# First batch of a Fourier filter: rows laid out from SBUF to SBUF, the last inverse rows moved straight to the first chunk's tile, ten crosswise filter steps by DMA

## The chip, the core and the metric

The kernel runs on one core of a Trainium2 chip. The metric is device time in microseconds (us), the median over the runs of one program. Engines are named as the profile names them: PE (matmuls), DVE (VectorE), ACT (ScalarE), POOL (GpSimd), SP (SyncE, which here only issues transfers). Transfers issued by SP and by ACT share the core's 16 DMA engines.

## The reference, cut to what matters

```python
def _attn_ref(x, filt_r, filt_i):                  # x: 8 x 3072 x 256
    X = np.fft.rfft(x, axis=1)
    Y = X * (filt_r + 1j * filt_i)[None]
    return np.fft.irfft(Y, n=x.shape[1], axis=1).astype(np.float32)

def _moe_ref(x, w_a, w_b, w_out):                  # d_ff = 1536
    return ((x @ w_a) * (x @ w_b) @ w_out).astype(np.float32)

reference = _moe_ref(_attn_ref(x).reshape(8 * 3072, 256), w_a, w_b, w_out)
```

The weights arrive as float64 and are converted to float32 parts on the chip, by integer work on DVE, ACT and POOL.

## The kernel before

A transform of length 3072 is done as 128 x 24. Forward stage one (`first_s1` in the first batch, `s1` later) multiplies by a 128-wide table for each of 24 columns n; the result is laid out anew so that a 24-point transform over n can run with (q, n) on 96 partitions; stage two (`first_s2`) does that transform and multiplies by the filter; the first inverse stage (`first_is1`) turns back; its rows go through a DRAM array `td` to a tile `tt`, in which 128 rows of one chunk stand together; the second inverse stage (`is2`) makes the first operand of the matrix part. Then the matrix part runs, six chunks a batch, with six visits (p) a chunk, and batches 1 to 7 have their transforms threaded between its matmuls. Only the first batch has nothing to hide behind: its transform stands in front of everything. The change touches this front.

The front in order. FRONT loads the table (`first_const`) and the input (`first_x`, six groups of four columns). `first_s1(i)`, i = 0 to 11, takes two columns each; eight of the twelve need their input split in two parts, `xh` by ACT and `xl` by POOL (`first_parts`). DVE copies each result back over the input tile (L526), and SP writes it to a DRAM array `z0` (L528, L530). `keep_warm` keeps PE busy with idle matmuls meanwhile. `between` then loads filters (`first_f`, 4 rows of 32 at a time, three tiles in turn) and reads `z0` back crosswise (`first_z`, eight groups g of four, six tiles in turn). The loop runs n = 0 to 18: `first_s2(n)` and, three steps behind, `first_is1(n-3)`. A step of `first_s2` multiplies its PSUM result by the filter (y) and by the filter with its two halves of 64 partitions exchanged (v). For nine of the 16 steps ACT makes the exchanged copy (`first_swap`, "w" in LOOP, two copies of 64 partitions); for the other seven DVE does v in two pieces (L584, L585). `first_is1` evicts by ACT (L598) and ACT stores pairs to `td` (L602, the last two one by one, L600). `first_tt` then loads `tt` by SP, two transfers for the first eight rows and two for the last eight.

The order of all this is written out by hand, engine by engine in program order: each engine and each issuing queue works through its own instructions in turn, and a wait blocks what stands behind it. The weight conversion is threaded in by the strings LOOP, TAIL, POST, LAST: for conversion number k, L loads raw words (SP), f takes the fields (DVE, L298, L299), p the power (ACT, L305, L306), s the sign (DVE, L311), g the high part (ACT, L318), l the low part (DVE, L321), v the value (POOL, L332), c the combination (POOL, L339), h the two float32 parts (ACT L350, POOL L351). Four raw tiles are used in turn.

A transfer raises one of eight completion semaphores, which are used in turn; an issue first waits for the earlier transfer on its own semaphore (`DMAHW0` to `DMAHW7` in the order rows).

Of the kernel before, what the change touches and what calls it, by code (L numbers as in the profile page):

```python
# [9 lines left out]
F32 = mybir.dt.float32  # L10
F32R = mybir.dt.float32r
# [9 lines left out]
NB = 32  # L21
# [64 lines left out]
def _tables():  # L86
# [98 lines left out]
    s1f = s1[[0, 12, *range(1, 12)]].transpose(1, 0, 2)  # L185
# [5 lines left out]
    for kind in range(2):  # L191
        for h in range(2):
            fi[64 * h:64 * h + 64, kind] = (1, -1)[h] * inv[kind, 0:64]
            fi[64 * h:64 * h + 64, 2 + kind] = inv[kind, 64:128]
    return [np.ascontiguousarray(a, np.float32) for a in (s1c, gc, fc, fl, ic, sc, s1f, ff, fi)]
# [23 lines left out]
def fft_filter_bilinear_kernel(ctx: ExitStack, tc, x, x0, filt, fny, filt0, fny0, wa, wb, wo, s1c, gc, fc, fl, ic, sc, s1f, ff, fi, out):  # L219
# [46 lines left out]
    def give_weights(p, where):  # L266
        wab[p] = [[where.tile([128, 7, 128], F32R, name=f"w{m}{h}{p}") for h in "hl"] for m in "ab"]

    for p in range(NP - LATE):
        give_weights(p, const)  # L270
    wo_h = [const.tile([128, 2, D], F32R, name=f"woh{p}") for p in range(NP)]
    wo_l = [const.tile([128, 2, D], F32R, name=f"wol{p}") for p in range(NP)]
# [6 lines left out]
    cut = pw.tile([128, 2], F32, name="cut")  # L279
    filts = [const.tile([128, 2, 2, D], F32, name=f"filt{i}") for i in range(2)]  # L280
# [85 lines left out]
    z0 = drc.tile([128, N2, D], F32, name="z0")  # L366
# [104 lines left out]
    def is1(b, i):  # L471
# [4 lines left out]
        nc.scalar.dma_start(out=td[b][i].rearrange("q n j d -> (q n) j d"), in_=t)  # L476


# [11 lines left out]
    def first_parts(i):  # L490
        g, h = divmod(i, 2)
        if i >= NI or i in WHOLE:
            return
        xt = held["x0", g][:, 2 * h:2 * h + 2]
# [6 lines left out]
    def first_x(g, parts=1):  # L501
        xt = fr.tile([128, 4, D], F32, name="x0", tag="in", bufs=6)
        xv = x0[:, 4 * g:4 * g + 4]
# [3 lines left out]
        held["x0", g] = xt  # L507

    BANKS = ((ps_h, "y"), (ps_h, "z"), (ps_o, "po0"), (ps_o, "po1"))

    def first_s1(i):
        g, h = divmod(i, 2)
        xt, sf = held["x0", g][:, 2 * h:2 * h + 2], held["sf"]
# [26 lines left out]
    def first_f(g):  # L540
        f = [*filts, more][g % 3].rearrange("p a n d -> p (a n) d")
        nc.sync.dma_start(out=f, in_=filt0[:, 4 * g:4 * g + 4])
# [479 lines left out]
```

## Time and profile before

| | us |
|---|---|
| median of 3 runs | 2463.68 (2462.14 to 2464.55) |
| the profiled execution | 2464.96 |
| its span, first to last instruction | 2463.2 |
| PE busy in the span | 2420.0 (98%) |
| DVE, ACT, POOL busy | 1780.7, 1405.0, 1223.0 |
| end of the last copy of stage one | 22.49 |
| start of the first matmul of `first_s2` | 30.39 |
| end of the last eviction of `first_is1` | 82.75 |
| start of the first eviction of `is2` | 90.00 |
| start of the matrix part's first matmul | 91.07 |

The page's 40 slices, of 61.6 us each, show PE at 70 to 89% in the first three and at 90% or more in all that follow. So the view to read is one by stages of the front, then the chain of waits through it, then the instructions in order of time.

### The profile page before, as it was taken

How to read it: one execution, taken by the hardware profiler on the slowest of the kernel's cores; microseconds unless marked ns; L12 is line 12 of the kernel's file. 1: busy time of each engine (PE TensorE's matmuls, PEld its weight loads, DVE VectorE, ACT ScalarE, POOL GpSimd, SP SyncE). 2: the span in 40 equal slices, each digit the busy share in tenths (PEclk: the TensorE clock that was granted, in tenths of full speed). 3: DMA queues.
4: the chain of work that ended last, by engine and by line, in shares of the span. 5: the costliest groups of instructions: out<-in, count | busy, mean ns of one | idle time of the engine just before them, and what ended most of it. 6: DMA issues, size and time to landing. Idle time of an engine off the chain costs nothing.

```text
span 2463.2 us, 46508 instructions
## 1 busy us (share of the span) xinstructions
PE 2420.0 (98%) x17478; PEld 2263.9 (92%) x17478; DVE 1780.7 (72%) x2511; ACT 1405.0 (57%) x2480; POOL 1223.0 (50%) x926
## 2 busy tenths in 40 slices
PE   7889999999999999999999999999999999999999
PEld 3588999999999999999999999999999999999998
DVE  6775996569955798568976589656996569955554
ACT  5755555555556555565555555565555655555454
POOL 4765454545545554454545545454454545534333
PEclk9999999999999999999999999999999999999999
DMA  9437442544334443245523454145432444310100
GB/s 303 160 127 239 148 134 71 171 143 142 116 102 142 152 154 114 88 146 160 159 80 112 157 158 139 63 145 166 142 121 78 161 144 149 108 39 22 44 22 18
DMA packets 209397, 310.21 MB, mean 126 GB/s; under 512 B 19186, under 2 KB 119476, under 8 KB 209092
## 3 DMA queue, kind: packets, MB, share of 16 engines
q1 hardware_dynamic: 166580, 230.55, 30.3%
q10 hardware_dynamic: 42592, 76.70, 8.9%
q8 instruction: 137, 2.24, 0.4%
q14 instruction: 88, 0.72, 0.1%
HBM read 202.31 MB, written 108.45 MB: 126 GB/s over the span
## 4 chain that ended last, share of the span: by engine, by line
PE 93%; DMA 2%; issue 2%; ACT 1%; DVE 1%; POOL 1%; SPq 0%; ACTq 0%; POOLq 0%; DVEq 0%
PE x L226 30%; PE po L226 30%; PE z L226 15%; PE y L226 7%; PE ps L635 3%; PE ps L226 3%; PE ps L441 2%; PE ps L442 2%; DMA filt<-in_filt 1%; PE ps L556 0%; POOL xl L393 0%; PE ps L524 0%; DMA zf<-z 0%; DVE g L678 0%; DMA gt<-in_gc 0%
## 5 line engine op out<-in xcount | busy, mean ns | idle before, releaser
L687 POOL TENSOR_TENSOR gl<-g,gh 128x512 fp32r<-128x512 f32 x574 | 745.1, 1301 | 788.8 <-ACT gh L686 762.5
L678 DVE TENSOR_TENSOR g<-c 128x512 f32<-128x512 f32 x576 | 509.1, 884 | 271.1 <-ACT c L968 134.0
L968 ACT COPY c<-x 128x512 f32<-128x512 f32 x288 | 169.2, 587 | 688.0 <-PE x L226 685.1
L686 ACT CAST gh<-g 128x512 fp32r<-128x512 f32 x576 | 357.1, 620 | 52.8 <-PE po L226 26.7
L226 PE MATMUL po<-gh,woh 128*128 128x512 f32 x1152 | 369.5, 388 | 2.6 <-DVE filt L706 2.6
L226 PE MATMUL po<-gl,woh 128*128 128x512 f32 x1152 | 359.8, 380 | 0.0
L226 PE MATMUL po<-gh,wol 128*128 128x512 f32 x1152 | 359.8, 380 | 0.0
L226 PE MATMUL x<-ah,wah 128*128 128x256 f32 x1152 | 316.8, 275 | 7.0 <-ACT c L932 4.5
L226 PE MATMUL x<-al,wah 128*128 128x256 f32 x1152 | 317.1, 275 | 0.1
L226 PE MATMUL x<-ah,wal 128*128 128x256 f32 x1152 | 316.9, 275 | 0.0
L226 PE MATMUL x<-ah,wbh 128*128 128x256 f32 x1152 | 316.9, 275 | 0.0
L226 PE MATMUL x<-al,wbh 128*128 128x256 f32 x1152 | 316.9, 275 | 0.0
L226 PE MATMUL x<-ah,wbl 128*128 128x256 f32 x1152 | 316.9, 275 | 0.0
L957 DVE TENSOR_TENSOR c<-x,c 128x512 f32<-128x512 f32 x288 | 197.9, 687 | 155.3 <-PE x L226 149.9
L226 PEld LDWEIGHTS po<-gl,woh 128*128 128x128 f32 x1152 | 217.3, 189 | 32.6 <-DVE gl L687 0.4
L226 PEld LDWEIGHTS po<-gh,wol 128*128 128x128 f32 x1152 | 218.3, 190 | 29.3
L226 PEld LDWEIGHTS x<-ah,wah 128*128 128x128 f32 x1152 | 219.5, 191 | 26.0 <-ACT c L932 5.9
L226 PEld LDWEIGHTS x<-al,wah 128*128 128x128 f32 x1152 | 219.6, 191 | 15.3 <-DVE al L646 0.3
L656 POOL TENSOR_TENSOR al<-t,ah 128x512 fp32r<-128x512 f32 x96 | 146.3, 1544 | 152.3 <-ACT ah L655 152.3
L226 PEld LDWEIGHTS x<-ah,wal 128*128 128x128 f32 x1152 | 221.3, 192 | 0.0
L226 PEld LDWEIGHTS x<-ah,wbh 128*128 128x128 f32 x1152 | 221.3, 192 | 0.0
L226 PEld LDWEIGHTS x<-al,wbh 128*128 128x128 f32 x1152 | 221.3, 192 | 0.0
(145 smaller groups left out, 6067.4 us busy)
## 6 DMA issues: line engine op xcount, KB each, us to landing
z<-zh ACTq DMA_DIRECT2D x112, 256.0 KB, 2.5
filt<-in_filt SPq DMA_DIRECT2D x112, 256.0 KB, 2.6
zth<-z SPq DMA_DIRECT2D x112, 256.0 KB, 3.0
tt<-td SPq DMA_DIRECT2D x94, 256.0 KB, 3.9
out<-ot SPq DMA_DIRECT2D x47, 512.0 KB, 3.0
td<-t ACTq DMA_DIRECT2D x114, 192.0 KB, 2.1
xt<-in_x SPq DMA_DIRECT2D x84, 256.0 KB, 4.2
st<-s1d SPq DMA_DIRECT2D x84, 256.0 KB, 2.7
```

Of the source, the lines that this page charges most:

```text
L226: nc.tensor.matmul(out, w, m, **kw)
L441: nc.tensor.matmul(out, w[:, 0], hi, start=True, stop=False)
L442: nc.tensor.matmul(out, wl[:, 0], lo, start=False, stop=True)
L635: nc.tensor.matmul(to, tt[:, n, 128 * k:128 * k + 128], gt[:, n].rearrange("p (k a) -> p k a", k=2), start=True, stop=True)
L656: nc.gpsimd.tensor_tensor(out=al[:, 3 + i:5 + i], in0=t[:, i:i + 2], in1=f32(ah[:, 3 + i:5 + i]), op=ALU.subtract)
L678: nc.vector.tensor_tensor(out=gt, in0=g[:, :, 0], in1=g[:, :, 1], op=ALU.mult)
L686: nc.scalar.copy(out=gh, in_=gt)
L687: low.tensor_tensor(out=gl, in0=gt, in1=f32(gh), op=ALU.subtract)
L957: nc.vector.tensor_tensor(out=c1[:, 1], in0=bx, in1=c1[:, 1], op=ALU.add)
L968: nc.scalar.copy(out=c1[:, 0], in_=bx)
```

## The change

- `first_z` no longer reads `z0`, which is gone. The input tile is one tile, `first_in`, of 24 columns, and group g is filled by four transfers from SBUF to SBUF, each from 4 partitions (24 columns of 1 KB) to 96 partitions of 1 KB: 32 transfers, all issued after the last copy of stage one. For g = 0 and 1 every second one is issued by ACT, the rest by SP. The targets are weight tiles that aren't written yet (`zs`). The columns of the stage one table are permuted on the host so that the four partitions of a transfer stand 32 apart.
- The exchanged filter is needed for all 16 steps: steps 0 to 5 by ACT as before, steps 6 to 15 by a transfer of 256 KB from a filter array with a third block of 64 rows (`first_w`), three buffers in turn. The seven steps with two pieces on DVE are gone.
- `first_is1` keeps its rows, from the third pair on, in columns of `first_in`, and the rows of `td` are ordered by chunk (in all batches; `load_td` reads them so). For steps 12 to 15 the 16 rows of chunk 0 go by two small transfers each straight into `tt`, without `td`; only steps 8 to 11 are left for the second `first_tt`.
- Smaller: ACT's table is loaded ahead of the data (`warm`); the pieces of the table load are 4, 4 and 5 columns instead of 3, 5 and 5; two filters are loaded before the first raw words; `keep_warm` 8 and 6 become 4 and 5; "f1 p1" moves from before the loop into its step 0; "h6" moves from TAIL to step 16 of the loop; the first low part in `is2` of chunk 0 goes from POOL to DVE.

```diff
-    s1f = s1[[0, 12, *range(1, 12)]].transpose(1, 0, 2)
+    s1f = s1[[0, 12, *range(1, 12)]].reshape(13, N1, 8, 4, 4).transpose(1, 0, 4, 3, 2).reshape(N1, 13, 128)
...
+    zs = [f32(whole).rearrange("p m h k f -> p (m h k f)")[:, 1024 * i:1024 * (i + 1)].rearrange("p (j d) -> p j d", d=D) for i in range(3)]
+    zs += [f32(t).rearrange("p h f d -> p (h f) d") for t in wo_b[:0:-1]]
...
-        td[b] = dr.tile([NJ, 4, N2, 2, D], F32, name="td", tag="td")
+        td[b] = dr.tile([NJ, NC, 4, 4, 2, D], F32, name="td", tag="td")
...
         nc.vector.tensor_copy(out=xt, in_=ps)
-        if g == NI // 2 - 1:
-            nc.sync.dma_start(out=z0[:, 2 * i:2 * i + 2], in_=xt)
-        elif h:
-            nc.sync.dma_start(out=z0[:, 4 * g:4 * g + 4], in_=held.pop(("x0", g)))
...
-    def first_z(g, parts=1):
-        zt = fr.tile([128, 4, D], F32, name="zf", tag="in", bufs=6)
-        zv = z0.rearrange("(j q) n d -> j (q n) d", q=4)[4 * g:4 * g + 4].rearrange("j p d -> p j d")
-        for n in range(parts):
-            part = slice(4 * n // parts, 4 * (n + 1) // parts)
-            nc.sync.dma_start(out=zt[0:96, part], in_=zv[:, part])
+    def first_z(g):
+        queues = (nc.sync, nc.scalar if g < 2 else nc.sync)
+        zt = zs[g]
+        zv = first_in.rearrange("(q m g) n d -> g m q n d", m=4, g=8)[g]
+        for m in range(4):
+            queues[m % 2].dma_start(out=zt[0:96, m], in_=zv[m])
...
+    def first_w(i):
+        if not swapped:
+            swapped.append(p2.tile([128, 3, 2, D], F32, name="fs", tag="al"))
         g, h = divmod(i, 2)
+        w = held["w", i] = swapped[0][:, i % 3]
+        if i < SWAPPED:
+            for a, b in ((0, 64), (64, 0)):
+                nc.scalar.copy(out=w[a:a + 64], in_=held["f0", g][b:b + 64, 2 * h:2 * h + 2])
+        else:
+            nc.sync.dma_start(out=w, in_=filt0[64:192, 2 * i:2 * i + 2])
...
-            nc.vector.tensor_tensor(out=v[0:64], in0=ps[64:128], in1=f[0:64], op=ALU.mult)
-            nc.vector.tensor_tensor(out=v[64:128], in0=ps[0:64], in1=f[64:128], op=ALU.mult)
+        nc.vector.tensor_tensor(out=v, in0=ps, in1=held.pop(("w", i)), op=ALU.mult)
...
+            if g < 2:
+                held["t0"] = fr.tile([96, 2, 2, D], F32, name="t0", tag="t")
+            else:
+                held["t0"] = first_in[0:96, 4 * g - 8:4 * g - 4].rearrange("p (h j) d -> p h j d", h=2)
...
+        near = 16 if i >= DIRECT else 0
+        if near:
+            tt = held["t", 0, 0][0][8 * i:8 * i + 8].rearrange("(q j) n d -> j q n d", j=2)
+            for j, queue in enumerate((nc.sync, nc.scalar if i == NJ - 1 else nc.sync)):
+                queue.dma_start(out=tt[j], in_=t[0:16, h, j])
...
+        between = [(lz, 0), (lz, 1), (steps, BETWEEN), (first_w, 0), (first_w, 1), load, (lz, 2), (lf, 2), (first_w, 2), (lz, 3), load, (lz, 4), load, (lz, 5), (lz, 6), (lz, 7)]
+        ISSUE = {0: ((first_w, 3),), 1: ((lf, 3), (first_w, 4),), 2: ((first_w, 5),), 3: ((first_w, 6), (lf, 4),), 4: ((first_w, 7),), 5: ((first_w, 8), (lf, 5),), 6: ((first_w, 9),), 7: ((first_w, 10), (lf, 6),), 8: ((first_w, 11),), 9: ((first_w, 12), (lf, 7),), 10: ((first_w, 13),), 11: ((first_w, 14),), 12: ((first_w, 15),)}
```

SP's queue where stage one ends, before: `z_122` is the DRAM array `z0`, `zf` the tile that is read back, `filt_118` a filter tile, `raw` the weight words. The writes end, and the reads wait for all of them.

```order
L528 DMA z_122<-x_150 128x512 [waits DMAHW5_49,DVE_49]
L528 DMA z_122<-x_150 128x512 [waits DMAHW6_49,DVE_49]
L288 DMA raw<-in_wb 128x2x512 [waits DMAHW7_49]
L542 DMA filt_118<-in_filt 128x1024 [waits DMAHW0_49]
L550 DMA zf<-z_122 96x2x256 [waits DMAHW4_49,DMAHW3_49,DMAHW5_49,DMAHW2_49,DMAHW6_49,DMAHW1_49,PE_49]
L550 DMA zf<-z_122 96x2x256
L542 DMA filt_119<-in_filt 128x1024
```

SP's queue now, at the end of the 32 transfers (`x_109` is `first_in`, `wo_88` a weight tile, `fs` the exchanged filter):

```order
L550 DMA wo_88<-x_109 96x1x256 [waits DMAHW3_49]
L550 DMA wo_88<-x_109 96x1x256 [waits DMAHW4_49]
L550 DMA wo_88<-x_109 96x1x256 [waits DMAHW5_49]
L550 DMA wo_88<-x_109 96x1x256 [waits DMAHW6_49]
L542 DMA filt_101<-in_filt 128x1024 [waits DMAHW7_49,DVE_49,Activation_49]
L569 DMA fs<-in_filt 128x512 [waits DMAHW0_49,DVE_49,Activation_49]
L542 DMA filt_102<-in_filt 128x1024 [waits DMAHW1_49]
L569 DMA fs<-in_filt 128x512 [waits DMAHW2_49,DVE_49,Activation_49]
L294 DMA raw<-in_wo 128x2x512 [waits DMAHW3_49]
```

The write and the read have become one transfer each, and the filter of group 3 (`filt_101`) and all exchanged filters by DMA stand behind the last of them.

ACT in the loop about step 7, before: exchanged copies (L569) stand among the evictions (L598).

```order
L598 COPY t_403<-ps 96x512 [waits PE_49]
L602 DMA td<-t_403 96x2x512 [waits DMAHW2_49,Activation_49]
L569 COPY fs<-filt_119 64x512 [waits DMAHW6_49]
L569 COPY fs<-filt_119 64x512
L318 ACTIVATE sc<-t 128x512 [waits DVE_49]
L305 ACTIVATE sc<-sc,cut 128x512 [waits DVE_49]
L306 ACTIVATE sc<-sc,cut 128x512 [waits Activation_49]
L598 COPY t_453<-ps 96x512 [waits DMAHW5_49,PE_49]
```

ACT at the same place now:

```order
L596 COPY t_390<-ps 96x512 [waits PE_49]
L603 DMA td<-t_390 96x2x512 [waits DMAHW4_49,Activation_49]
L324 ACTIVATE sc<-t 128x512 [waits DVE_49]
L311 ACTIVATE sc<-sc,cut 128x512 [waits DVE_49]
L312 ACTIVATE sc<-sc,cut 128x512 [waits Activation_49]
L596 COPY x_109<-ps 96x512 [waits DMAHW5_49,DMAHW3_49,DMAHW6_49,DMAHW1_49,DMAHW7_49,DMAHW0_49,PE_49]
L596 COPY x_109<-ps 96x512 [waits PE_49]
```

The copies are gone, and the eviction of step 4 of `first_is1`, which writes into `first_in`, waits for transfers out of it on six semaphores.

ACT where the front ends, before: the last evictions, each with a store to `td`, then "h6" (two casts) and the conversions of TAIL.

```order
L598 COPY t_647<-ps 96x512 [waits PE_49]
L600 DMA td<-t_647 96x512 [waits Activation_49]
L350 CAST wah_91<-m 128x896 [waits Pool_49]
L350 CAST wbh_93<-m 128x896
L318 ACTIVATE sc<-t 128x512 [waits DVE_49]
L305 ACTIVATE sc<-sc,cut 128x512 [waits DVE_49]
L306 ACTIVATE sc<-sc,cut 128x512 [waits Activation_49]
L318 ACTIVATE sc<-t 128x512 [waits DVE_49]
L350 CAST woh_100<-t 128x512 [waits Pool_49]
```

ACT at the same place now:

```order
L596 COPY x_109<-ps 96x512 [waits PE_49] x2
L601 DMA tt<-x_109 4x4x256 [waits DMAHW2_49,Activation_49]
L603 DMA td<-x_109 80x2x512 [waits DMAHW4_49]
L324 ACTIVATE sc<-t 128x512 [waits DVE_49]
L311 ACTIVATE sc<-sc,cut 128x512 [waits DVE_49]
L312 ACTIVATE sc<-sc,cut 128x512 [waits Activation_49]
L324 ACTIVATE sc<-t 128x512 [waits DVE_49]
L356 CAST wo_88<-t 128x512 [waits Pool_49]
```

The transfer into `tt` comes straight behind the last eviction, and the two casts of "h6" stand earlier in the program.

## Rows read from the trace of the kernel before

**Rows 1.** Windows by stage: stretch, length, engine busy us (instructions), PE clock, DMA share, GB/s.

```profile
core 0: us, PE busy (x) PEld busy (x) DVE busy (x) ACT busy (x) POOL busy (x), PEclk, DMA share, GB/s
0.00:22.50 22.50, 13.74 (x34) 8.33 (x34) 10.38 (x19) 7.26 (x13) 10.69 (x12) 1.00 0.87 319
22.50:30.40 7.90, 7.14 (x17) 2.97 (x17) 2.62 (x5) 3.78 (x6) 0.00 (x0) 1.00 1.03 312
30.40:50.00 19.60, 14.94 (x39) 6.33 (x39) 16.50 (x27) 10.95 (x20) 5.36 (x6) 1.00 1.07 293
50.00:66.00 16.00, 14.38 (x33) 5.32 (x34) 15.80 (x24) 12.59 (x21) 13.55 (x10) 1.00 0.98 296
66.00:82.75 16.75, 15.23 (x36) 5.73 (x35) 15.65 (x27) 13.61 (x24) 9.91 (x10) 1.00 0.73 226
82.75:91.10 8.35, 6.27 (x27) 3.41 (x25) 2.77 (x6) 5.73 (x11) 6.58 (x4) 1.00 0.62 199
91.10:130.00 38.90, 32.86 (x222) 29.47 (x223) 30.60 (x51) 25.69 (x46) 28.24 (x19) 0.96 0.41 143
```

**Rows 2.** The chain that ended last, in order of time: start us, us, what.

```profile
22.51 2.98 DMA z<-x
25.56 4.79 DMA zf<-z
...
36.23 10.01 DMA filt<-in_filt
...
82.78 2.13 DMA td<-t
...
85.69 3.00 DMA tt<-td
...
90.00 0.59 ACT x L643
...
93.29 1.28 POOL al L656
```

**Rows 3.** Timeline, stage one: start us, us, engine, line, operation, count, idle before.

```profile
7.16 1.28 ACT L487 ACT_TABLE_LOAD   x1 [7.16 <-DMA sf<-in_s1f]
...
8.66 0.35 SPq L808 DMA_DIRECT2D icf<-in_fi  x1
...
9.46 10.48 POOL L498 TENSOR_TENSOR xl<-x,xh 128x512 fp32r<-128x512 f32 x8 [9.02 <-ACT xh L497]
...
17.48 5.01 DVE L526 COPY x<-ps 128x512 f32<-128x512 f32 x7
```

**Rows 4.** Timeline, from the end of stage one to the last eviction.

```profile
22.40 0.69 DVE L298 TENSOR_SCALAR sc<-raw 128x512 int32<-128x512 int32 x1
...
23.81 0.66 ACT L306 ACTIVATE sc<-sc,cut 128x512 int32<-128x512 f32 x1
...
30.39 2.08 PE L556 MATMUL ps<-zf,fcf 96*128 96x256 f32 x6 [0.72 <-DMA zf<-z]
...
48.64 0.68 DVE L580 TENSOR_TENSOR y<-ps,filt 128x512 f32<-128x512 f32 x1
...
82.17 0.58 ACT L598 COPY t<-ps 96x512 f32<-96x512 f32 x1 [0.40 <-PE ps L556]
```

**Rows 5.** Groups by line in 30.4 to 82.75: busy us, mean ns, idle before.

```profile
L569 ACT COPY fs<-filt 64x512 f32<-64x512 f32 x14 | 8.6, 617 | 5.9 <-DMA filt<-in_filt 5.4 <-ACT t L598 0.4
...
L585 DVE TENSOR_TENSOR v<-ps,filt 64x512 f32<-64x512 f32 x5 | 3.4, 683 | 0.1
```

**Rows 6.** SP's issues of the reads of `z0`: ns min/median/max, first and last start.

```profile
L550 SPq DMA_DIRECT2D zf<-z x9: 342/432/465, 25.6 to 62.0; - x9
```

**Rows 7.** DMA queues in 300 to 2300 us: packets, MB, share of 16 engines' time.

```profile
q1 hardware_dynamic: 136800, 179.68, 29.3%
q10 hardware_dynamic: 36176, 65.09, 9.3%
```

More of the change, by code (lines that the diff above doesn't have):

```diff
@@ L194, in _tables @@
             fi[64 * h:64 * h + 64, 2 + kind] = inv[kind, 64:128]
+    ic, fi = (a.reshape(*a.shape[:-1], 4, NC, 4).swapaxes(-3, -2).reshape(a.shape) for a in (ic, fi))
     return [np.ascontiguousarray(a, np.float32) for a in (s1c, gc, fc, fl, ic, sc, s1f, ff, fi)]
@@ L266, in give_weights @@
     def give_weights(p, where):
-        wab[p] = [[where.tile([128, 7, 128], F32R, name=f"w{m}{h}{p}") for h in "hl"] for m in "ab"]
+        whole = where.tile([128, 2, 2, 7, 128], F32R, name=f"wab{p}")
+        wab[p] = [[whole[:, m, h] for h in range(2)] for m in range(2)]
+        return whole
     for p in range(NP - LATE):
-        give_weights(p, const)
-    wo_h = [const.tile([128, 2, D], F32R, name=f"woh{p}") for p in range(NP)]
-    wo_l = [const.tile([128, 2, D], F32R, name=f"wol{p}") for p in range(NP)]
+        whole = give_weights(p, const)
+    wo_b = [const.tile([128, 2, 2, D], F32R, name=f"wo{p}") for p in range(NP)]
+    wo_h, wo_l = ([t[:, h] for t in wo_b] for h in range(2))
+    zs = [f32(whole).rearrange("p m h k f -> p (m h k f)")[:, 1024 * i:1024 * (i + 1)].rearrange("p (j d) -> p j d", d=D) for i in range(3)]
+    zs += [f32(t).rearrange("p h f d -> p (h f) d") for t in wo_b[:0:-1]]
     fct = const.tile([128, 3, 128], F32R, name="fct")
@@ L279, in fft_filter_bilinear_kernel @@
     cut = pw.tile([128, 2], F32, name="cut")
+    warm = pw.tile([128, 2], F32, name="warm")
     filts = [const.tile([128, 2, 2, D], F32, name=f"filt{i}") for i in range(2)]
@@ L556, in first_turn @@
                 nc.tensor.matmul(ps[:, j0:j1], w[q][:, kind], m[:, j0:j1], start=q == 0, stop=q == len(ins) - 1)
-    swapped = {}
-    def first_swap(i):
+    swapped, SWAPPED = [], 6
+    def first_w(i):
+        if not swapped:
+            swapped.append(p2.tile([128, 3, 2, D], F32, name="fs", tag="al"))
         g, h = divmod(i, 2)
-        f = held["f0", g][:, 2 * h:2 * h + 2]
-        if not swapped:
-            swapped["w"] = p2.tile([128, 3, 2, D], F32, name="fs", tag="al")
-        w = held["w", i] = swapped["w"][:, len(swapped) % 3]
-        swapped[i] = True
-        for a, b in ((0, 64), (64, 0)):
-            nc.scalar.copy(out=w[a:a + 64], in_=f[b:b + 64])
+        w = held["w", i] = swapped[0][:, i % 3]
[4 more added lines that the diff above has]
+            nc.sync.dma_start(out=w, in_=filt0[64:192, 2 * i:2 * i + 2])
     def first_s2(i):
@@ L787, in steps @@
                     load_weights()
-                elif what[0] == "w":
-                    first_swap(int(what[1:]))
                 else:
@@ L823, in fft_filter_bilinear_kernel @@
         nc.vector.memset(cut[:, 1:2], float(255 << 23))
+        nc.scalar.copy(out=warm, in_=cut)
         for what, *args in FRONT:
@@ L841, in fft_filter_bilinear_kernel @@
                 first_s2(n)
-            if n % 2 and n // 2 + 3 < NJ // 2:
-                first_z(n // 2 + 3)
-            if n % 2 and n // 2 + 3 < NJ // 2:
-                first_f(n // 2 + 3)
+            for what, *args in ISSUE.get(n, ()):
+                what(*args)
             if n >= 3:
```

91 lines of the change are left out of this document (44 added, 47 removed).

## The prediction, made before the changed kernel was run

> **What bounds the kernel now.** I read the page first: PE is busy 98% of the span, so only the front before the matrix part has time to give. The windows by stage [rows 1] say how much: in the first 91.1 us PE misses 8.8 us in stage one, 0.8 between the stages (filled with idle matmuls, so that stretch is 7.9 us without any use), 7.8 us in the loop (4.7 + 1.6 + 1.5) and 2.1 plus some 5 us of idle matmuls at its end. Next the chain of waits in order of time [rows 2]. It has four places: the write of `z0` and its reading back (2.98 and 4.79 us), waits for filters in the loop (the longest 10.01 us), the store to `td` and the load of `tt` (2.13 and 3.00 us), and the split in `is2` by POOL (1.28 us). Last the timeline, for what stands ahead of each. In the loop no engine is free: of 52.4 us (30.4 to 82.75) DVE works 48.0, PE 44.6, and the DMA engines are at a share of about 1 until 66 [rows 1]. So the loop hangs on several limits at once, and taking one away gives little more than the distance to the next.
>
> **The change, part by part.** The sum is made against the profiled execution, 2464.96 us, which lies 1.28 above the median of the three runs.
>
> *Stage one.* POOL's eight splits run as one block of 10.48 us from 9.46, which starts late: ACT's first cast waits for the second table piece until 7.16 and then for 1.28 us of table load [rows 3]. Now the table is loaded ahead, and the first cast needs only the first piece. The first split goes ahead, but the second needs input group 1; the issue of `icf` that waits for it starts at 8.66 [rows 3]. With one copy of about 0.6 us on ACT the second split starts at 9.3 instead of 9.46 + 1.31 = 10.77. That is 1.5 us for the whole block. Bounds: 1.2 (only the load is saved) and 2.9 (if group 1 doesn't hold it). Stage one then ends at 21.0, not 22.49 (17.48 + 5.01, rows 3).
>
> *The layout.* Before, 7.9 us from the last copy to 30.39. Now two transfers must land for step 0, one from SP, at once, and one from ACT, which first does the power of conversion 0: DVE's fields at 22.40, ACT's second ACTIVATE over at 24.47 [rows 4], 2.0 us after the last copy. An issue by SP takes 0.43 us [rows 6], and a landing lies between the 2.13 us of the `td` store and the 2.98 of the `z0` write [rows 2], so it is 2.0 + 2.1 to 3.0, with the issue 4.1 to 5.4. I take 4.5: step 0 at 25.5. This saves 3.4 us (2.5 to 3.8).
>
> *The loop.* DVE loses seven instructions of 0.683 us, 4.8 us [rows 5]; "f1" comes into the loop with about 1.1. ACT loses six of 18 copies of 0.617, 3.7 us, and the 11 us in which its queue stood still for filters, of which 5.4 is in the row [rows 5]. So by DVE the loop shrinks by 3.7 us to 48.7. What takes some of it back: SP's queue. Behind stage one stand 28 transfers, three weight loads and a filter, 32 issues of 0.43 us = 13.8 us, or nearer 18 if an issue from four partitions takes longer than the row's longest. Filter 3 is issued at 35 to 39 and lands, like the loads in the chain, up to 10.01 us later [rows 2]; y of step 6 wants it at about 42 (48.64 in rows 4, less 4.9, less some). I count 0 to 5 us, and take 1.7. Exchanged filters have three buffers, so each has three steps to arrive in; PE's share of a step is 44.6/16 = 2.8 us, three are 8.4 us, and most landings fit into it. Loop: 2.0 us saved (-3 to +6).
>
> *The end.* From the last eviction's end, 82.75 [rows 4], to ACT's first eviction of `is2` at 90.00 [rows 2] is 7.25 us: store, load, matmuls. Now one transfer stands there, 0.6 + 2.1 to 3.0, and 1.2 us of matmuls: 3.9 to 4.8. But ACT itself has two issues (0.6), four conversion steps of about 0.6 to 0.66 and a cast of 0.6 before that eviction, with a sign on DVE (0.69) between: 4.4 us. I take 4.4, saved 2.8 (1.0 if a conversion is late, 3.4 if none is). "h6" costs nothing in the loop: its 1.9 us on ACT take the room of the copies; without them ACT would be later by that much at the end.
>
> *`is2`.* The low part by DVE takes 0.7 us, not POOL's 1.28 [rows 2]: 0.6 us. The new order of `td` leaves pieces of 1 KB as they were: nothing, and the visits hide the loads in any case.
>
> *After it* conversions and matrix part keep their order, so the shift is handed on. From 91.1 to 130 PE works 32.9 of 38.9 us beside a DVE at 30.6 and POOL at 28.2 [rows 1]; an earlier start could lose or win 2 us there.
>
> Sum: 1.5 + 3.4 + 2.0 + 2.8 + 0.6 = 10.3 us. 2464.96 - 10.3 - 1.28 = 2453.4; I say **2453.5**. With the bounds the forecast's own range is 2445 to 2460.
>
> **The rivals.**
>
> *Slower: the 32 transfers run on a part of the DMA engines.* Each has only four source partitions. The large transfers of the front have 32 to 128 rows on both sides, so no row shows what four do. If only four of 16 engines work on them, 3072 packets of 1 KB are 768 for each. The two queues took 0.293 x 16 x 2000/136800 = 68.5 ns for a packet of 1.31 KB and 0.093 x 16 x 2000/36176 = 82 ns for 1.80 KB [rows 7], scaled 47 to 53 ns a KB; at the loop's load, a share of 1.07 at 293 GB/s [rows 1], 60 ns. So 36 to 46 us, and 6 to 7 more for the 2 MB of weights and filter between (at about 300 GB/s), from 21.0 to 63 to 74. Two things stand behind the last: filter 3 in SP's queue, for y of step 6, and ACT's eviction of step 4 in `first_is1`, into the tile that is still read. At 53 ns step 6 has its y at about 69 instead of 48.64. After it PE has some ten inverse and nine forward steps, 27 us with waits, so the last eviction ends at 96 instead of 82.75. Less 3.4 us for the end and `is2`, that is 10 us lost: 2474 (47 to 60 ns, with waits: 2467 to 2485). It decides from some 40 us for the layout: up to there the loop's own pace hides it.
>
> This is also what the Trainium skill says. "DMA: Bandwidth & Descriptors", in the section on why a DMA increments its semaphore by 16, has a transfer use the largest number of engines, up to 16, that divides the slowest dimension of both sides; of 4 and 96 that is 4, and always the same ones. By that rule this rival is the forecast and the time 2474. The trace can't say: it has no transfer of such a shape.
>
> For the rival: the shape is new, and both waits are in the order. Against it: no row shows a transfer on a part of the engines, the reads of 1 KB and the weights between the stages come at 312 GB/s together [rows 1], and even 40 us of transfers would be read in time by a loop of 50 us, were it not for what is queued behind. I give it 0.25.
>
> *No difference: DVE waits for the exchanged filters.* ACT's copies are replaced by ten transfers of 256 KB in a stretch where DMA is at a share of 0.98 to 1.07 [rows 1], and a load can take 10.01 us to land [rows 2]. With three buffers a step then takes (10.0 + 0.4 + 0.7)/3 = 3.7 us, not 2.8; over ten steps 9 us, which is the gain of the other parts: 2463, and the bytes are the same 293 GB/s that the loop had. It decides from a landing of about 7.3 us on. For it: the sum of bytes hardly falls, `z0` moved twice and now once, but 2.6 MB of filters come. Against it: the layout is over by the time the exchanged filters begin, and then the 1 KB reads are gone from the mix. I give it 0.15.
>
> *It doesn't do what it says* would be a wait left on the old path; the order shows none, and I give that nothing of its own.
>
> **How the numbers follow.** Forecast 0.60, slower rival 0.25, no difference 0.15. A measurement of this kernel can tell about 0.2%, 4.9 us. The forecast lies beyond that but for its upper end; what it gives up there the second rival's lower side gives back. So faster 0.60, same 0.15, slower 0.25. A range for 8 in 10 reaches from the forecast's lower end, 2445, into the slower rival until half of it is in: **2445 to 2476**.
>
> **What would show it.** Right: first split at about 6.5 and stage one over by 21; first matmul of `first_s2` at 25 to 26; all 32 transfers landed by 40 and eviction of step 4 not waiting for them; `is2`'s first eviction within 5 us of the last one of `first_is1`, at 79 to 81 instead of 90.0. The slower rival would show as a landing of the last layout transfer beyond 60, DMA share near 0.25 to 0.5 while they run, and PE, DVE and ACT idle together about steps 4 to 6. The second rival would show as DVE waiting for `fs` at every step. The forecast is wrong, with all of that right, if the matrix part from 91 to 260 us later takes back what it got.

## The result: 2487.66 us, slower by 0.93%, and the profile after

The changed kernel takes 2487.66 us (median of 4 runs, 2483.97 to 2489.75) against 2464.11 for the kernel before beside it: a ratio of 1.0093, 95% interval 1.0076 to 1.0109, 23.5 us lost. The forecast was 2453.5 and its range ended at 2476. The side it came out on is that of the slower rival, priced at 2474. The profiled run took 2488.81 us, with a span of 2487.0. Two of the nine runs of experiment 8 below came in a slow state, at 3117 and 3574 us, and the median given there is that of the other seven.

First the windows by stage of the kernel after; columns as in [rows 1], cut where its own stages change.

```profile
core 0: us, PE busy (x) PEld busy (x) DVE busy (x) ACT busy (x) POOL busy (x), PEclk, DMA share, GB/s
0.00:22.00 22.00, 14.57 (x34) 8.41 (x34) 11.34 (x19) 7.74 (x14) 10.70 (x12) 1.00 0.77 267
22.00:26.00 4.00, 3.70 (x8) 1.44 (x8) 1.57 (x3) 1.32 (x2) 0.00 (x0) 1.00 0.16 31
26.00:34.00 8.00, 2.56 (x6) 1.10 (x6) 1.81 (x3) 5.16 (x9) 0.00 (x0) 0.74 0.43 124
34.00:38.00 4.00, 2.52 (x4) 0.50 (x2) 0.84 (x2) 0.51 (x2) 0.00 (x0) 0.50 0.27 95
38.00:52.00 14.00, 9.12 (x19) 4.19 (x18) 5.13 (x10) 3.03 (x6) 1.27 (x1) 0.74 0.55 167
52.00:56.00 4.00, 0.97 (x2) 0.40 (x3) 4.00 (x7) 3.39 (x6) 2.12 (x3) 0.50 0.28 97
56.00:66.00 10.00, 10.00 (x20) 3.86 (x18) 2.67 (x5) 4.68 (x7) 7.54 (x6) 0.77 0.43 134
66.00:82.75 16.75, 4.97 (x9) 1.66 (x8) 7.29 (x13) 3.60 (x7) 2.26 (x3) 0.64 0.91 310
82.75:91.10 8.35, 8.35 (x19) 3.38 (x18) 8.09 (x14) 6.47 (x10) 7.30 (x6) 0.90 0.95 318
```

In [rows 1] the DMA engines are at a share of 0.98 to 1.07 and 293 to 312 GB/s from 22.5 to 66. Here they are at 0.27 and 95 GB/s where hardly anything but the row transfers runs (34 to 38, 52 to 56): 0.27 x 16 is 4.3 engines. A share of 0.27 at 95 GB/s is 46 ns for a packet of 1 KB on one engine, so the engines that work are not slow; the others have nothing to do. PE pays twice: it works 5.0 of 16.75 us in 66 to 82.75 (15.2 before), and where it has waited its granted clock is at 0.50, the 1.2 GHz level (34 to 38, 52 to 56).

The issues of the row transfers (duration in ns as min/median/max, then first and last start):

```profile
L550 SPq DMA_DIRECT2D wo<-x x20: 520/1012/2442, 38.2 to 62.7; - x20
L550 SPq DMA_DIRECT2D wab<-x x8: 519/626/1736, 22.0 to 37.1; - x8
L550 ACTq DMA_DIRECT2D wab<-x x4: 539/1426/1847, 23.3 to 26.8; - x4
```

The issue of a read of `z0` took 432 ns [rows 6]; these take 1012 as a median for the later ones: SP's queue goes at the pace of the four engines (run 5 shows this by itself). The last is issued at 62.7. Then the chain that ended last (start, us, what):

```profile
26.72 10.38 DMA raw<-in_wb
...
62.75 0.79 SPq L550
...
63.65 0.87 SPq L542
...
67.05 10.29 DMA raw<-in_wo
77.44 0.71 DVE sc L304
78.17 0.67 ACT sc L311
...
79.46 0.59 ACT x L596
80.09 21.30 PE ps L556 x44
...
105.91 1.07 ACT x L596 x2
107.00 0.74 ACTq L601
...
109.05 2.37 DMA tt<-x
...
111.51 3.55 PE ps L642 x16
```

Filter 3 is issued at 63.65 behind the last transfer, and step 6 gets its product at 71.76 (48.64 in [rows 4]), after DVE has waited 13.1 us for that filter. Behind the filters in SP's queue the weights `in_wo` are issued at 67.05 and land 10.29 us later; DVE's and ACT's conversion of them stands ahead of ACT's eviction of step 4 (L596, 79.46), for which PE has waited 12 us. From 80.09 on all is there, and the loop runs through in 26.9 us. Its last eviction ends at 106.97, not 82.75; the first of `is2` starts at 113.38, not 90.00. That is 23.4 us, and the whole program is 23.5 us longer.

### The profile page after: what moved, and what is told of

Its sections match the earlier page's. It is cut to its first block, busy times and chain, and to the rows that moved or that the text cites. A ratio compares the mean times of both kernels' runs of the same rounds, so it can differ in the third digit from the quotient of the medians.

```text
span 2487.0 us, 46522 instructions
## 1 busy us (share of the span) xinstructions
PE 2426.3 (98%) x17468; PEld 2267.5 (91%) x17468; DVE 1778.0 (71%) x2505; ACT 1402.5 (56%) x2475; POOL 1221.6 (49%) x925
## 4 chain that ended last, share of the span: by engine, by line
PE 92%; DMA 2%; DVE 2%; SPq 1%; ACT 1%; issue 1%; POOL 1%; ACTq 0%; POOLq 0%; DVEq 0%
PE x L227 30%; PE po L227 29%; PE z L227 15%; PE y L227 7%; PE ps L642 3%; PE ps L227 3%; PE ps L446 2%; PE ps L447 2%; SPq L550 1%; PE ps L556 1%; DMA raw<-in_wb 0%; DMA raw<-in_wo 0%; POOL xl L398 0%; DMA x<-in_x 0%; DVE g L686 0%
## 5 line engine op out<-in xcount | busy, mean ns | idle before, releaser
L227 PE MATMUL x<-ah,wab 128*128 128x256 f32 x4608 | 914.4, 275 | 6.8 <-ACT c L940 4.6
L227 PEld LDWEIGHTS x<-ah,wab 128*128 128x128 f32 x4608 | 768.5, 192 | 25.4 <-ACT c L940 5.7
L227 PE MATMUL x<-al,wab 128*128 128x256 f32 x2304 | 634.2, 275 | 0.0
L227 PE MATMUL po<-gh,wo 128*128 128x512 f32 x2304 | 618.2, 384 | 1.9 <-DVE filt L714 1.9
L227 PE MATMUL z<-ah,wab 128*128 128x256 f32 x2304 | 481.0, 275 | 0.3 <-ACT ah L662 0.3
L227 PEld LDWEIGHTS x<-al,wab 128*128 128x128 f32 x2304 | 441.3, 192 | 15.1
L227 PEld LDWEIGHTS po<-gh,wo 128*128 128x128 f32 x2304 | 407.0, 190 | 46.3 <-DVE filt L714 2.1
L227 PEld LDWEIGHTS z<-ah,wab 128*128 128x128 f32 x2304 | 396.6, 192 | 0.8 <-ACT ah L662 0.7
L694 ACT CAST gh<-g 128x512 fp32r<-128x512 f32 x576 | 357.0, 620 | 52.2 <-PE po L227 26.7
L227 PE MATMUL po<-gl,wo 128*128 128x512 f32 x1152 | 359.5, 380 | 0.0
L227 PE MATMUL z<-al,wab 128*128 128x256 f32 x1152 | 317.4, 276 | 2.3 <-POOL al L664 1.9
```

Source lines behind the costliest of these rows:

```text
L227: nc.tensor.matmul(out, w, m, **kw)
L694: nc.scalar.copy(out=gh, in_=gt)
```

## The experiments

Each ratio is to the kernel before on the same chip, with its 95% interval in brackets. A table at the end of this section sets the profiles side by side.

**1. The layout undone alone.** Row order, `z0` and its writes and reads as in the kernel before, into the change's tiles:

```diff
+            nc.sync.dma_start(out=z0[:, 2 * i - 2:2 * i + 2], in_=first_in[:, 2 * i - 2:2 * i + 2])
...
-        for m in range(4):
-            queues[m % 2].dma_start(out=zt[0:96, m], in_=zv[m])
+        zv = z0.rearrange("(j q) n d -> j (q n) d", q=4)[4 * g:4 * g + 4].rearrange("j p d -> p j d")
...
+            nc.sync.dma_start(out=zt[0:96, part], in_=zv[:, part])
```

> The changed kernel with one part undone: the rows go from SBUF to z0 in DRAM and back as in the kernel before (row order of stage one too), now into the same tiles as the 32 transfers; everything else of the change stays. If the 32 transfers of four source partitions are the whole loss: no stretch of the front at a DMA share near 0.26 any more, first step of first_s2 back at 29.5 to 31, filter 3 landed before 45, last eviction of first_is1 at 78 to 84 instead of 106.5, and 2455 to 2463 us, that is at or a little below the kernel before. If the crosswise filters by DMA or the inverse rows in the first chunk's tile lose the time, the last eviction stays beyond 95 and the time above 2475.

2469.0 us, ratio 1.0011 (1.0003 to 1.0020). Of the loss of 0.93%, 0.82 points go with this one part: about 20 us. Last eviction 86.39, first of `is2` 92.28. The first theory holds for the size, but not for the rest: the kernel is not below the one before. No run has the layout from SBUF to SBUF on more than four engines in this kernel; that their number is what costs rests on the measurement of run 5.

**2. The eviction's wait taken away.** All inverse rows go to the rotating tiles.

```diff
-            if g < 2:
-                held["t0"] = fr.tile([96, 2, 2, D], F32, name="t0", tag="t")
-            else:
-                held["t0"] = first_in[0:96, 4 * g - 8:4 * g - 4].rearrange("p (h j) d -> p h j d", h=2)
+            held["t0"] = fr.tile([96, 2, 2, D], F32, name="t0", tag="t")
```

> The changed kernel, but the inverse rows of all steps go to the two rotating tiles, as the kernel before had them, instead of into the tile that the 32 transfers read; so ACT's eviction of step 4 no longer waits for the transfers. My prediction named that wait as one of two that count. By the trace of the changed kernel ACT was held until 78.2 by a conversion whose weights landed at 77.4, long after the transfers, so: no change, 2484 to 2491 us, eviction of step 4 still at about 79. If the wait on the transfers does carry the loss: PE's 12.6 us before 80.1 go, 2472 to 2480.

2488.27 us, 1.0089 (1.0074 to 1.0103); the eviction of step 4 at 80.67. No change: one of the two waits that my rival named is there in the order, but another always ends later.

**3. Nothing queued behind them.** Groups 4 to 7 of the transfers are issued within the loop, behind filters 3 to 6, with the rotating tiles of run 2.

```diff
-... (lz, 4), load, (lz, 5), (lz, 6), (lz, 7)]
+... load]
-1: ((lf, 3), (first_w, 4),), ... 7: ((first_w, 10), (lf, 6),)
+1: ((lf, 3), (first_w, 4), (lz, 4)), ... 7: ((first_w, 10), (lf, 6), (lz, 7))
```

> The same 32 transfers on as few engines, but those of groups 4 to 7 are issued within the loop, one group with each filter from 3 on, behind filter 3, and not all ahead of it; the inverse rows in rotating tiles as in the run before (else they would overwrite rows not yet read). If what stands behind the transfers in SP's queue is the loss: filter 3 is issued at about 40 and not 63.7, the loop hides most of the transfers, last eviction at 85 to 93 instead of 106.5, 2464 to 2474 us. If the transfers themselves set the loop's pace, wherever they stand (3.0 MB at 95 GB/s are 33 us of four engines that weights and filters need too): last eviction beyond 97, 2478 us or more.

2486.0 us, 1.0081 (1.0068 to 1.0094); last eviction 104.77, `is2` at 110.68. The other named wait falls too: against run 2 the place in SP's queue is worth some 2 us of 23.5 (4 by the two profiles), with overlapping intervals. The chain of this run shows what it is instead:

```profile
25.56 10.33 DMA raw<-in_wb
...
61.86 7.35 DMA fs<-in_filt
69.22 10.27 DMA raw<-in_wb
79.56 8.54 DMA fs<-in_filt
...
88.84 6.72 DMA fs<-in_filt
```

Each load of weights or of a filter is spread over all engines, also over the four that work at the transfers, and it has landed only when its last share has. So in the kernel after a load of 512 KB takes 10.38 us (from 26.72) though the DMA share is 0.43 and then 0.27. Its packets show it, in 29 to 32 and in 32 to 37.2:

```profile
DMA packets 397, 0.58 MB, mean 195 GB/s; under 512 B 18, under 2 KB 205, under 8 KB 397
DMA packets 402, 0.46 MB, mean 88 GB/s; under 512 B 18, under 2 KB 338, under 8 KB 402
```

The row transfers move packets of 1 KB, the load 256 of 2 KB. Of these, 192 (397 - 205) begin in the first 3 us, and the other 64 (402 - 338), a quarter, as it would be for four engines of 16, need the next 5 us. In run 1 loads take as long (9.03 and 12.51 us in its chain), but there all engines are at a share of 1.03 to 1.11.

**4. Other rows, as many of them.** Stage one leaves its rows so that a transfer reads four neighbouring partitions, not four that are 32 apart.

```diff
-        zv = first_in.rearrange("(q m g) n d -> g m q n d", m=4, g=8)[g]
+        zv = first_in.rearrange("(g m q) n d -> g m q n d", m=4, g=8)[g]
```

> The changed kernel with another order of rows in stage one: the four source partitions of a transfer are neighbours (4j to 4j+3) and not 32 apart. The count of partitions, the bytes and the order of issue stay. If the number of source partitions sets how many DMA engines work: the same share of 0.25 to 0.27 and 90 to 100 GB/s while only these transfers run, last of them issued at 61 to 66, 2482 to 2493 us. If it is which partitions they are (rows that come out of the same part of SBUF), the rate moves by more than a tenth, either way, and the time by more than 5 us.

One run of 2514.39 us, 26.7 above the changed kernel. Both theories were put as either-or, and both are half right. Two windows in which hardly anything but the row transfers runs on the DMA engines:

```profile
46.00:50.00 4.00, 2.83 (x7) 0.87 (x5) 0.00 (x0) 1.73 (x3) 0.00 (x0) 1.00 0.23 51
82.00:89.00 7.00, 0.00 (x0) 0.00 (x0) 0.00 (x0) 0.00 (x0) 0.00 (x0) 0.75 0.24 52
```

The share is that of four engines again (0.23, 0.24), but the rate is 51 and 52 GB/s and not 95: a packet takes some 75 ns and not 46. It is a single run.

**5. The transfer by itself.** Six groups of eight transfers of 96 KB ahead of the changed kernel; only the source partitions differ.

```diff
+        for kind in ("32 apart", "neighbours", "8 apart", "8 rows", "16 rows", "96 rows"):
+            for k in range(8):
+                nc.vector.memset(zs[k][0:96, 0], 0.0)
+            for k in range(8):
+                nc.sync.dma_start(out=zs[k][0:96, 0], in_=rows)
```

> The changed kernel with the disputed cost measured by itself ahead of it: six groups of eight transfers from SBUF to SBUF, each transfer 96 rows of 1 KB into 96 partitions, that differ only in where the 96 rows come from: 4 partitions 32 apart (as in the change), 4 neighbours, 4 partitions 8 apart, 8 partitions 16 apart, 16 partitions 8 apart, 96 partitions. Before each group DVE clears the destinations, so that the groups stand apart. If the number of source partitions sets how many of the DMA engines work: a share of about 0.25, 0.25, 0.25, 0.5 and more for the last two, and the last two groups are limited by their issues (8 of about 0.5 us) alone. 4 rows 32 apart come at 90 to 100 GB/s (8.3 us for a group), neighbours at 45 to 55 (16 us). 4 rows 8 apart: 90 to 105 GB/s if 24 GB/s is what one engine gives, 140 or more if the place of the rows in SBUF still held back the rows 32 apart. If the number of source partitions doesn't count, the three last groups are no faster than the first.

The windows within the six groups, in that order (by the packets, each group's 768 of 1 KB end at 20.7, 39.1, 47.8, 55.0, 60.1 and 65.5):

```profile
9.00:21.00 12.00, 0.00 (x0) 0.00 (x0) 2.35 (x9) 0.00 (x0) 0.00 (x0) 1.00 0.25 66
22.00:39.00 17.00, 0.00 (x0) 0.00 (x0) 1.90 (x7) 0.00 (x0) 0.00 (x0) 1.00 0.23 44
41.00:47.00 6.00, 0.00 (x0) 0.00 (x0) 1.63 (x6) 0.00 (x0) 0.00 (x0) 1.00 0.27 96
48.00:53.00 5.00, 0.00 (x0) 0.00 (x0) 1.63 (x6) 0.00 (x0) 0.00 (x0) 1.00 0.47 103
57.00:60.00 3.00, 0.00 (x0) 0.00 (x0) 1.18 (x6) 0.00 (x0) 0.00 (x0) 1.00 0.67 160
61.00:65.00 4.00, 0.00 (x0) 0.00 (x0) 0.00 (x0) 0.03 (x1) 0.00 (x0) 1.00 0.52 142
```

The share goes by the number of source partitions: 0.23 to 0.27 with four, 0.47 with eight. With 16 and 96 it is 0.67 and 0.52; there the issues, 0.62 to 0.7 us for 96 KB, set the pace. By the Trainium skill, "DMA: Bandwidth & Descriptors", section "Why a DMA increments its semaphore by 16 and not by 1", the engines are the largest number up to 16 that divides the slowest dimension of both sides. The shares agree for 4 and 8.

The rate goes by which partitions they are as well: 66 GB/s 32 apart, 44 for neighbours, 96 when 8 apart, all on four engines; and eight partitions 16 apart keep twice the engines busy for 103. The Trainium skill, "SBUF — State Buffer", section "Door 1: The DMA port swizzle (why `[64,N]` ≈ `[32,N]`)", puts four neighbours on one port, four rows 32 apart on two, four rows 8 apart on four and these eight on four. The order of the four rates agrees. Its figure for four ports, 104 GB/s with a transfer of 1 MiB, agrees with the 103. The 96 says less, since four engines that never wait give nearly as much whatever the ports (4 KB in 46 ns are 89 GB/s). The page's figure for partitions 0 to 3, on one port, 27.6 GB/s, does not agree: 44 here and 52 in run 4. One thing stays open: 32 apart gave 66 GB/s here and 95 to 97 in the later stretches of the changed kernel, where loads stand between the transfers in the queue; there two ports did not hold them back.

**6. The better rows in the kernel.** The changed kernel with rows 8 apart.

```diff
+        zv = first_in.rearrange("(u q m) n d -> u m q n d", q=4, m=8)
+            queues[m % 2].dma_start(out=zt[0:96, m], in_=zv[(4 * g + m) // 8][(4 * g + m) % 8])
```

> The changed kernel, its 32 transfers from SBUF to SBUF kept, with one more order of rows in stage one: the four source partitions of a transfer are 8 apart, where the measurement by itself gave 95 GB/s and not 65 (32 apart) or 45 (neighbours), at the same share of about a quarter. If the place of the rows counts beside their number: the first transfers land earlier, last of them issued at 50 to 59 instead of 62.8, 2470 to 2483 us. If in the kernel the number alone counts (there the rows 32 apart came at up to 98 GB/s later on): 2485 to 2491 us. In either case it stays slower than the kernel before.

2484.46 us, 1.0074 (1.0059 to 1.0088); last transfer issued at 57.9, last eviction 101.88. In the first 3 us of the transfers nearly the same share moves almost twice as much; the kernel after, then this run:

```profile
23.00:26.00 3.00, 2.71 (x7) 0.93 (x5) 0.69 (x1) 0.92 (x2) 0.00 (x0) 1.00 0.21 41
22.00:25.00 3.00, 3.00 (x9) 1.31 (x7) 0.69 (x1) 0.92 (x2) 0.00 (x0) 1.00 0.23 76
```

Later both move 95 to 96 GB/s at 0.27 where only such transfers run. The time lies between the two forecasts: the profile says 5 us, the runs say 3 to 5, and their intervals overlap a little. The number of engines remains the larger cause (20 us in run 1).

The next runs go by way of `z0` and ask why the rest of the change is no gain.

**7. The reads of `z0` within the loop** (groups 3 to 7, as in the kernel before).

```diff
-... (lz, 3), load, (lz, 4), load, (lz, 5), (lz, 6), (lz, 7)]
+... load, load]
-1: ((lf, 3), (first_w, 4),), 3: ((first_w, 6), (lf, 4),), ...
+1: ((lz, 3), (lf, 3), (first_w, 4),), 3: ((lz, 4), (first_w, 6), (lf, 4),), ...
```

> The way through DRAM as in the run before last, and the loads of groups 3 to 7 issued within the loop, one with each filter, as in the kernel before; the other parts of the change stay. With all loads issued ahead of the loop the weights landed late (9.0 to 12.5 us), and the last eviction was at 86.4, 3.6 us later than in the kernel before. If the crowd ahead of the loop is that cost: last eviction at 79 to 83 and 2457 to 2463 us. If the ten filters that now come a second time by DMA are the cost: no change, 2466 to 2470.

2469.15 us, 1.0016 (1.0008 to 1.0025): no change; last eviction 87.77.

**8. Without the direct inverse rows** (run 7, DIRECT = 16 instead of 12).

> The same without the last inverse rows in the first chunk's tile: all of them go by way of td. My prediction gave that part 2.8 us; in the trace of the changed kernel the stretch from the last eviction to the first of is2 was 6.4 us and not 7.25, so 0.9. If that reading is right: 0 to 2 us slower than the same kernel with it. If the prediction's step was right: 2.5 to 4 us slower.

2471.70 us, 1.0030 (1.0019 to 1.0041), against 1.0016 with them: 2.6 us slower by the medians and 3.4 by the ratios, intervals overlapping. From the last eviction to the first of `is2` it takes 10.07 us, with the direct rows 6.0, in the kernel before 7.25. The last eviction itself came 2.7 us earlier than in run 7, so the first of `is2` is only 1.4 later. The number is that of the prediction's step, but the comparison is with a worse end than the old one: this run stores the last two steps' rows in one piece behind the last eviction, where the kernel before stored the first of them earlier.

**9. All exchanged filters by ACT** (run 7, SWAPPED = 16 instead of 6).

> The same as the last but one, but all sixteen exchanged filters by ACT's copies, none by DMA: 2.6 MB less to load, 20 copies of 0.62 us more on ACT. My prediction gave the loop 2 us for taking these steps off ACT and DVE (DVE's part stays here). If the second loading of filters costs the loop more than ACT's copies do: faster than the kernel with DMA by 2 us or more. If the copies cost more: slower by 2 us or more, ACT's queue waiting for filters as in the kernel before.

2471.11 us, 1.0028 (1.0017 to 1.0038). By the medians 2 us slower than run 7, with overlapping intervals, last eviction 89.94. Sixteen by ACT is no better than ten by DMA; the kernel before had nine by ACT and seven on DVE.

**10. The front as before.** Run 7, filters 0 and 1 behind the writes of `z0`, eight idle matmuls, not four. **11.** Run 7 with the eight idle matmuls alone.

```diff
-            (lx, 3), (lx, 4), (lx, 5), (small_tables,), (lf, 0), load, (lf, 1),
+            (lx, 3), (lx, 4), (lx, 5), load, (small_tables,),
-    WARM = 4, 5
+    WARM = 8, 5
```

> As the run with the loads in the loop (rows by way of DRAM), but two more things as in the kernel before: filters 0 and 1 are issued behind the writes of z0 and no longer ahead of them, and eight idle matmuls, not four, stand between the stages. In that run the last write of z0 took 7.6 us to land (2.98 in the kernel before), first_s2 began at 31.8, and TensorE's clock fell to half while PE idled. What is left of the change: table load ahead, ten filters by DMA, direct inverse rows, low part by DVE. If the two are what the change still lost: first_s2 at 28.5 to 30.5, last eviction at 78 to 82.5, first of is2 at 84 to 88.5, 2454 to 2461 us, below the kernel before. If the filters that come twice are the loss: 2466 to 2470 us, no change.

> As the run with the loads in the loop, with eight idle matmuls and not four between the stages, the filters still ahead of the writes of z0: it tells the two apart. If the clock is the loss: 2460 to 2465 us. If it is the filters' place in the queue: within 1.5 us of 2469, since z0 comes back too late for PE anyway and the clock falls all the same.

2467.48 us (1.0006, 0.9997 to 1.0015) and 2467.12 (1.0007, 0.9998 to 1.0016): each is better than run 7 by some 2 us in the medians, with overlapping intervals; they are not told apart from each other, and neither is below the kernel before. In run 10 `first_s2` starts at 29.00, yet the last eviction is at 88.33. Its chain, and its window from 66 on, where [rows 1] has a share of 0.73:

```profile
37.09 10.43 DMA filt<-in_filt
47.54 11.96 DMA wo<-z
59.55 7.84 DMA fs<-in_filt
...
71.88 7.22 DMA fs<-in_filt
```

```profile
66.00:82.75 16.75, 14.23 (x28) 5.04 (x28) 12.87 (x22) 8.68 (x15) 9.10 (x9) 0.90 1.01 321
```

The loop hangs on loads from end to end, among them the filters that come a second time: DVE waits for those four times, 5.8 us in all.

**12. The filters as before.** Run 10, the exchanged filters nine by ACT and seven on DVE.

> Rows by way of DRAM, filters and idle matmuls as in the run with the front as before, and now the exchanged filters too as in the kernel before: nine by ACT's copies, seven steps with two half products on DVE, none loaded a second time. Left of the change: table load ahead and the first cast's smaller piece, the direct inverse rows, the low part by DVE, the tiles. In the run with the ten filters by DMA the DMA share stayed at 1.06, 1.06, 1.01 to 82.75 (1.07, 0.98, 0.73 in the kernel before) and the loop took 59.3 us, not 52.4. If the second loading of filters is the rest of the loss: share near 0.75 in 66 to 82.75, loop 51 to 54 us, last eviction at 80 to 83, first of is2 at 86 to 89, and 2459 to 2463 us, below the kernel before. If something else makes the loop longer (tiles, order of conversions): last eviction beyond 85, 2465 us or more.

2464.55 us, 1.0003 (0.9995 to 1.0012): level with the kernel before. The same window, and where the early start (28.23) went, in the timeline:

```profile
66.00:82.75 16.75, 15.92 (x36) 5.95 (x37) 16.52 (x26) 14.02 (x25) 12.17 (x11) 1.00 0.64 196
```

```profile
35.56 0.69 DVE L304 TENSOR_SCALAR sc<-raw 128x512 int32<-128x512 int32 x1 [4.52 <-DMA raw<-in_wb]
```

The share falls to 0.64, and the last eviction comes at 83.79, 4.5 us earlier than in run 10. In whole runs the step is 2.9 us by the medians, 0.7 by the ratios with overlapping intervals: that the second loading lengthens the loop is what this pair of profiles shows (59.3 and 55.6 us from first matmul to last eviction), and its price in whole runs is not told from nothing. In 66 to 82.75 DVE now works 16.5 of 16.75 us, so its wait of 4.52 us is not made up there.

**13. The same without the direct rows.**

> The same without the direct inverse rows: by way of td, in its new order. Left of the change: table load ahead, smaller first piece, low part by DVE. Against the run before it this is the worth of the direct rows where nothing crowds them. The pair with ten filters by DMA gave 3.6 us; by the end stretch of the kernel before, 7.25 against some 6.2 us, it is 1. So 1 to 4 us slower than the run with direct rows; about level with the kernel before (2460 to 2466).

2468.41 us, 1.0016 (1.0007 to 1.0024): 3.2 us behind run 12 by the ratios (3.9 by the medians, intervals overlapping a little), at the same longer end as run 8 (10.71 us).

**14. DVE's wait of run 12 taken away:** the second weights issued ahead of filter 0, as before.

```diff
-    BETWEEN = 's0 g0'
+    BETWEEN = 'L s0 g0 f1 p1'
-        0: 'f1 p1',
```

> The run with the filters as before, and the second piece of weights too is issued where the kernel before issues it, ahead of filter 0 and the first rows read back, with its first conversion step between the stages. In that run first_s2 began at 28.2 and not 30.4, but DVE then waited 4.5 us, until 35.6, for that piece, with the product of step 1 behind it, and the loop took 55.6 and not 52.4 us. If this wait is where the early start went: the product of step 1 at 31 to 33.5 and not 36.7, last eviction at 80 to 82 and not 83.8, first of is2 at 86 to 88, 2460 to 2463 us, just below the kernel before. If the loop is DVE's by its work alone (its wait only moves): last eviction at 83 to 85, 2464 to 2466.

2467.69 us, 1.0011 (1.0002 to 1.0020): not faster, and outside both forecasts. The product of step 1 comes at 34.14 and not 36.74, but the rows of `z0` are later (`first_s2` at 30.79), and the chain now has another load:

```profile
37.03 11.83 DMA filt<-in_filt
```

From 22.5 to 66 the DMA engines are at a mean share of 0.96 to 1.04 in runs 10 to 14. In these runs the order of the loads decides which engine waits, and what was taken ahead made something else late.

The profiles side by side, in us: first matmul of `first_s2`, end of the last eviction of `first_is1`, start of the first eviction of `is2`, and the profiled run's own time (medians and ratios stand above).

| kernel | first_s2 | last eviction | is2 | run |
|---|---|---|---|---|
| before | 30.39 | 82.75 | 90.00 | 2464.96 |
| after | 26.08 | 106.97 | 113.38 | 2488.81 |
| 1, layout by DRAM | 29.64 | 86.39 | 92.28 | 2469.52 |
| 2, rotating tiles | 24.85 | 108.40 | 114.70 | 2490.76 |
| 3, transfers in the loop | 24.93 | 104.77 | 110.68 | 2484.26 |
| 6, rows 8 apart | 24.55 | 101.88 | 108.42 | 2484.92 |
| 7, reads in the loop | 31.77 | 87.77 | 93.78 | 2469.29 |
| 8, no direct rows | 30.37 | 85.09 | 95.16 | 2473.04 |
| 9, filters by ACT | 30.05 | 89.94 | 97.09 | 2469.60 |
| 10, front as before | 29.00 | 88.33 | 94.38 | 2468.35 |
| 11, idle matmuls | 31.16 | 87.11 | 93.96 | 2467.97 |
| 12, filters as before | 28.23 | 83.79 | 89.86 | 2465.39 |
| 13, no direct rows | 27.66 | 82.80 | 93.51 | 2468.55 |
| 14, weights as before | 30.79 | 88.02 | 93.43 | 2469.20 |

## Why the prediction was wrong

**The choice.** The step that failed is the weighing: 0.60 for transfers on all engines, 0.25 for four, because no row had a transfer of such a shape. "Against it" I put that 40 us of transfers would be read in time by a loop of 50 us. Both halves are wrong. The absence of a row is no evidence for the cheap side, and the transfers are not alone: the loads of that loop use the same four engines (the packets in run 3's section).

In the sum the failed step stands in the loop's term. It charged the transfers with their issues alone, 13.8 or nearer 18 us for all 32, and nothing for the engines that carry them: filter 3 was to be issued at 35 to 39 and was issued at 63.65. (The bounds of the parts add up to 2447 to 2461, and not to the stated 2445 to 2460; nothing hangs on that.)

**The rival's price.** Its packet price was about right: 47 to 60 ns for 1 KB, against 46 measured, and the end of the layout at 63 to 74, against a last issue at 62.7 to 63.5 and last packets of 1 KB at about 70. y of step 6 came at 71.76, put at 69. The run from there, 27 us, was 26.9. What was missed stands between: the rival let PE go on at 69, but it went on at 80.1, when the weights of 77.44 were converted. 96 + 11.1 is the 107 that was measured, and with it the time goes from 2474 to 2485; the 2 us that the end did not save bring it to 2487. The two things "queued behind the last" do not carry it: runs 2 and 3 took them away for nothing and for some 2 us.

**Stage one**, put at 1.5 us saved: 0.5 in this profile (over at 21.96), and 0.5 to 2.6 in those of the other runs with the same work there, with 1.6 in the middle; so the size was right and this profile lies at the low end. The table load went as foreseen, but the second cast waited for input group 1 until 9.42, so the second split came at 10.12 and not 9.3.

**The layout**, put at a first matmul at 25.5: 26.08, before 30.39. The term was right for the first two transfers, and for nothing after: PE then waited 2.3 and 3.0 us for the next two (29.09, 32.83), and so on.

**The loop**, put at 2.0 us shorter: it took 80.9 us from 26.08 to 106.97, 28.5 longer. Without the transfers (run 10) it took 59.3, still 7.0 longer than the 52.4 before. Part of that is the second rival's mechanism: the exchanged filters whose landing is seen took 7.2 to 7.8 us against its condition of 7.3, DVE waited for four of the ten and not at every step, and without them (run 12) the loop took 55.6. What makes up the other 3.2 us is open. My reason against it, that the layout is over by then, has no test in run 10, which reads `z0` within the loop. In the changed kernel itself the mechanism did not show, all else being later.

**The end**, put at 4.4 us: 6.41, before 7.25. I made ACT's work the limit and counted one transfer. In the chain it is the transfers, and more than one of SP's stands behind the last eviction:

```profile
106.94 2.83 SPq L601 DMA_DIRECT2D tt<-x  x4
```

SP issues seven of the eight small transfers, and these four go one after the other. The last is issued at 109.05 and its rows are there at 111.42, 2.37 us later, which is what was put for one; ACT's own transfer was issued at 107.00. PE's eight products and ACT's eviction follow. So 0.8 us were saved, not 2.8; the 3 us of runs 8 and 13 are against a longer end, not against the old one. No run shares these issues out otherwise.

**`is2`'s low part on DVE** is right: 0.69 us at 117.41 where POOL took 1.28 [rows 2].

**That the shift is handed on** is right: the program's time less the start of the first eviction of `is2` is 2374.96 us before and 2375.43 after, so nothing of the 23.5 us has to be looked for behind it. In the 14 profiles of the table it is 2372.5 to 2377.9, a little wider than the 2 us either way that I allowed, so a single profile does not tell an effect of 1 to 3 us.

So the change's own accounts are: about 20 us lost by the layout, clear of all noise; the ten filters a loss of perhaps 1 to 3, and fewer idle matmuls and early filters perhaps 2, neither apart from noise in whole runs; and the table load, the direct rows and the low part together nothing that shows, since run 12 has them all and is level. No version here beats the kernel before.

## What to carry to other kernels

Before a transfer is reshaped, look how many partitions or rows its slowest dimension has on either side, not only at its bytes; a new shape on the critical path wants a measurement of eight such transfers by themselves. Count a slow transfer's cost at every load that shares its engines, since a load has landed only with its slowest share. Where the DMA share is about 1 over a stretch, an earlier start or another order of loads can move the wait and not remove it (runs 7 and 14); fewer bytes there took 3.8 us off the loop of run 12's profile.

## What was not expected of the hardware

An issue is not of fixed cost: for the same 96 KB it took 0.52 us at least and up to 2.44 while the engines were behind, so that SP's queue, and everything in it, ran at the pace of four engines. Run 5 has it by itself: the last five issues of a group took 7.30 us for rows 32 apart, 11.49 for neighbours, 5.00 for rows 8 apart and 3.11 with 16 partitions. Which partitions are read counts as much as a factor of two at nearly the same engine share (44 GB/s at 0.23, 96 at 0.27). And the clock made it worse: after PE had waited for rows (busy 2.6 of 8 us in 26 to 34) the granted clock was 0.50 in 34 to 38, and a pair of matmuls of 512 columns took 2.0 us where the later steps took 1.02.
